# Chunked linear attention and a max-out feed-forward: the feed-forward of chunks 4 to 11 over two chunks at a time

## The chip, the cores and the metric

One NeuronCore of a Trainium2 chip runs the whole program in one launch. The engines are TensorE (PE, matmuls, with its weight loads shown apart as PEld), VectorE (DVE), ScalarE (ACT), GpSimd (POOL) and SyncE (SP), which here only issues transfers. The metric is the device time of one execution in microseconds, taken over several executions; lower is better.

## The reference, cut to what matters

```python
# r, k, v: (4, 8, 768, 48); w, u: (8, 48)
for t in range(768):
    cur = einsum('bhd,bhe->bhde', u * k[t], v[t])
    y[t] = einsum('bhd,bhde->bhe', r[t], state + cur)
    state = w[:, :, None] * state + einsum('bhd,bhe->bhde', k[t], v[t])
x = y as (4 * 768 tokens, 384)
h = maximum(maximum(x @ w1, x @ w2), x @ w3)      # 384 -> 768
out = h @ w_out                                   # 768 -> 384
```

The weights of the feed-forward come as float64 and everything else as float32.

## The kernel before, in words

The 768 steps are cut into 12 chunks of 64. A chunk holds 64 steps of 4 batches, 256 tokens (TOK), and is worked on in two halves q, each of four heads. Within a chunk the recurrence is written as matmuls: scores of k and r (`scores`), masked to earlier steps (`mask`); values (`values`), which add scores times v and r times the incoming state; keys (`keys`), which with `into_state` make the state of the next chunk. These operands are split into a high and a low float16 part, each product of two operands being three matmuls (`three`, L410, PSUM pool psa, 64 or 48 columns). The stationary operands are block-diagonal tiles (`Block`: kb, ktb, vb, sb) that a transfer from one SBUF tile to another spreads out (`spread`, L320 and L321). So each half chunk has loads (feat, tok), scaling on POOL or DVE (L367, L386, L406), splitting on ACT and DVE (L333, L338, L340), spreads, matmuls, and at the end x of the chunk: `x_high` (ACT, L466) and `x_low` (DVE, L471), two tiles xh and xl of 128 x 3 x 256 in the float32r form.

The feed-forward of a chunk (`ffn`) takes x = xh + xl and weights split likewise. For each of six slices f of the hidden columns and each of the three matrices i, `up` makes nine matmuls (three parts of the inner dimension times three products) into a PSUM tile of the pool psm (4 buffers): 18 groups of nine. `first` (ACT, L499) copies the group i = 0 to a tile m, `least` (DVE, L503) takes the maximum with groups 1 and 2, `h_high` (ACT, L506) and `h_low` (POOL or DVE, L512) split the result into hh and hl. `down` then makes 3 x 18 matmuls, `leaving` (ACT, L535) copies each of the three output tiles to a tile io, and ACT issues its store (L874). All feed-forward matmuls have line L488; a chunk has 162 + 54 = 216 of them with 256 columns.

At the start 16 half blocks of weight words (float64, 576 KB each, tiles raw64, 4 buffers) are loaded and converted by ACT and DVE to a high and a low part that stay in SBUF. Near the end the same words are loaded a second time (`again`, L698) and vetted: `vet_words` (DVE, L264) and `vet_sum` (ACT, L268) check that each lies in the range in which the fast conversion holds; `check`, `count` and `verdict` join all such checks, and a slow general path (`general`) would run after the fast one if any failed.

The order of the work on every engine is written out ahead by a planner, `Plan`. Each step is announced with `do`: an engine, a modelled cost, what it reads, writes and takes from a pool, and a due time in chunks. `order` then goes through a model of the five engines: the step that can start earliest goes first, and among those that can start at about the same time the one with the lower due time. The due times are moved by SHIFT, by kind of step ("act m": ACT steps that make m), with two values, for dues up to 1.6 and later. Attention of chunk c + 1 is due at c and the feed-forward of chunk c also at c. On the chip each engine keeps the order so found and waits where an operand isn't there. SP issues all loads and spreads, in order.

```python
plan = Plan(dict(feat=2, tok=3, raw64=4, psa=4, psm=4, ..., xh=2, xl=2, m=3, io=3, hh=1, hl=1))
...
order = plan.order(dict(pe=0.5, dve=5.2, act=3.0, pool=13.0, sp=1.6))
for p in order:
    p["fn"]()
```

Of the kernel before, what the change touches and what calls it, by code (L numbers as in the profile page):

```python
# [18 lines left out]
P = 128  # L19
B, H, S, D = 4, 8, 768, 48  # L20
C = 64
# [16 lines left out]
class Plan:  # L38
# [6 lines left out]
    OPENING = 1.6  # L45
    SHIFT = {
        "act ah": (-5.31, -0.9), "act am": (2.08, 0), "act hh": (1.37, 0.4), "act his": (-0.69, 0), "act io": (-5.36, -2.55),
        "act kb": (-1.33, 0), "act kdh": (-2.9, 1.2), "act ktb": (1.56, 0), "act ktdh": (2.65, 0.45), "act m": (0.81, -0.9),
        "act odd": (0, 0.6), "act rh": (1.04, -0.85), "act sdh": (-5.26, 2.75), "act sq": (-6.83, 0.2), "act state": (-3.36, 0),
        "act tkt": (-0.31, 0), "act vb": (-2.77, 0), "act vdh": (-3.65, 2.05), "act xh": (1.12, -1.45), "act ztop": (-4.35, 0),  # L50
        "dve a": (4.95, 2.4), "dve al": (5.58, 0.7), "dve am": (-3.84, 0.85), "dve ends": (0, 0.45), "dve flag": (0, -2),
        "dve good": (0, -3), "dve hl": (2.63, -2.25), "dve kT": (6.29, 0), "dve kdec": (8.61, 0), "dve kdl": (-1.52, -0.15),
        "dve ktdl": (-3.55, 1.1), "dve lo": (-4.52, 0), "dve m": (-2.24, 0.3), "dve rT": (9.32, 0), "dve rl": (-2.27, 0.75),
        "dve sdl": (3.31, -0.15), "dve state": (-2.75, 1.5), "dve vdl": (4.98, 0.55), "dve vet": (0, -0.15), "dve word": (-1.81, 0),
# [10 lines left out]
    def do(self, due, eng, cost, fn, reads=(), writes=(), takes=(), size=0, near=0):  # L65
# [6 lines left out]
        late = due > self.OPENING  # L72
        due += self.SHIFT.get(kind, (0, 0))[late]
# [8 lines left out]
        self.todo.append(dict(n=n, due=due, eng=eng, cost=cost, fn=fn, need=need, takes=takes, size=size, near=near, kind=kind, late=late, touch={*reads, *writes, *new}))  # L82
# [68 lines left out]
def kernel(ctx, tc, feat, tok, wu, ut, ws, wo, cst, out):  # L151
# [9 lines left out]
    wld = ctx.enter_context(tc.tile_pool(name="wld", bufs=4))  # L161
# [57 lines left out]

    def load_weight(n, h, shift=0):  # L220

        raw = wld.tile([P, 4 * HN + 4], I16, name="raw64")
        src = (ws[n] if n < NF else wo[n - NF]).bitcast(I16)
        nc.sync.dma_start(out=raw[:, shift:shift + 4 * HN], in_=src[:, h * 4 * HN:(h + 1) * 4 * HN])
        return raw

# [44 lines left out]
    pw = wld.tile([P, NP, C + 1], F32, name="raw64")  # L271
# [261 lines left out]
    def leaving(ps, n):  # L533
        o = tmp.tile([P, n], F32, name="io", bufs=3)
        nc.scalar.copy(out=o, in_=ps)  # L535
        return o

    def xtile(n):
        return [xp.tile([P, NJ, n], F32R, name=f"x{s}") for s in "hl"]
# [36 lines left out]
    def general():  # L576
# [60 lines left out]
        with tc.For_i(0, NCH // 2, 1) as i:  # L637
            for b in range(B):
                xt = wld.tile([P, NJ, P], F32, name="raw64")
# [13 lines left out]
                x = xtile(P)  # L653
# [15 lines left out]
    plan = Plan(dict(feat=2, tok=3, raw64=4, psa=4, psm=4, rh=2, rl=2, am=2, a=2, ah=1, al=1, xh=2, xl=2, m=3, io=3, hh=1, hl=1))  # L669
# [7 lines left out]
    def helping(c, columns):  # L677
        return ("pool", 0.05 + 2.5e-3 * columns) if c > 2 else ("dve", dve(columns))

    def dve(columns):  # L680
        return 0.07 + 1.05e-3 * columns
# [4 lines left out]
    def weight(n, h, due):  # L686
# [5 lines left out]
        dma(due, fetch, 8 * P * HN, takes=[("raw64", w)])  # L692
# [5 lines left out]
    def again(n, h, due):  # L698
        w = ("vet", n, h)

        def fetch():
            T[w] = load_weight(n, h)

        dma(due, fetch, 8 * P * HN, reads=[("begun", int(due))], takes=[("raw64", w)])
# [99 lines left out]
    def leave_x(c, q, due):  # L804
        def x_hi():
            if q == 0:
                T["x", c] = [xp.tile([P, NJ, TOK], F32R, name="xh"), None]
            x_high(c, q, T["x", c][0])

        def x_lo():  # L810
            if q == 0:
                T["x", c][1] = xp.tile([P, NJ, TOK], F32R, name="xl")
            x_low(c, q, *T["x", c])

        hi, lo = ("xh", c), ("xl", c)
        do(due + 0.03, "act", 0.6 if q == 0 else 1.55, x_hi, reads=[("va", c, q)], **(dict(takes=[("xh", hi)]) if q == 0 else dict(writes=[hi])))
        do(due + 0.04, "dve", 0.62 if q == 0 else 1.7, x_lo, reads=[("va", c, q), hi], **(dict(takes=[("xl", lo)]) if q == 0 else dict(writes=[lo])))
# [18 lines left out]
    def ffn(c):  # L836
        x = [("xh", c), ("xl", c)]
        for f in range(NF):
            due = c + 0.11 * f
            for i in range(3):  # L840
                def mul(f=f, i=i):
                    T["up", c, f, i] = up(T["x", c], f, i, TOK)
# [133 lines left out]
```

## Time and profile before

| what | value |
|---|---|
| time, median of 3 runs | 414.87 us (414.4 to 414.98) |
| profiled execution: span | 413.4 us; no other time is given for it |
| PE busy | 393.2 us, 95% |
| DVE, ACT, POOL busy | 283.6 (69%), 256.1 (62%), 183.2 us (44%) |
| moved by the DMA engines | 90.08 MB, 218 GB/s on average |
| granted TensorE clock, mean | 0.998 |

The span goes from the first to the last instruction of the program. PE's busy time is that of matmuls that overlap in the engine's pipeline, so the spacing of matmuls is read from the chain and from the timeline, in which equal neighbours are merged: "160.53 11.75 PE psm L488 x99" is a stretch that begins at 160.53 us, lasts 11.75 us and holds 99 matmuls. A row of a group gives the busy time, the mean duration in ns, then the engine's idle time ahead of it with what ended it. A row of waits gives the sum, how often, and the longest.

### The profile page before, as it was taken

Reading aid. Unit: us, or ns where it says so; the run is one execution under the profiler, and the core shown is the slowest. Engines: PE = TensorE matmul, PEld = TensorE weight load, DVE = VectorE, ACT = ScalarE, POOL = GpSimd, SP = SyncE. Lnnn points to the kernel's source line nnn. Section 1 sums busy time; section 2 is a strip of 40 time slices with the busy share of each in tenths; the row PEclk is TensorE's granted clock in tenths of the full one; section 3 lists DMA queues with packets and bytes.
Section 4 is the critical chain, followed back from the end, with each engine's and each line's share of the span. In section 5 each row is a group of like instructions: output and inputs, shape, how many; then the busy total and the mean of one; then the engine's idle time right before and its main releaser. Section 6 shows DMA issues by size and latency. Waiting matters only on the chain.

```text
span 413.4 us, 11975 instructions
## 1 busy us (share of the span) xinstructions
PE 393.2 (95%) x4758; PEld 388.5 (94%) x4758; DVE 283.6 (69%) x550; ACT 256.1 (62%) x674; POOL 183.2 (44%) x180
## 2 busy tenths in 40 slices
PE   2869999999999999999999999999999999999996
PEld 2759999999999999999999999999999999999995
DVE  6888999988688766767667666567676596354240
ACT  5999987885766556456456456466456477265231
POOL 9000000298668754674664654754574551020120
PEclk9999999999999999999999999999999999999999
DMA  7899998889799997786785786785885996886101
GB/s 286 320 314 212 255 307 285 223 224 293 207 276 239 248 226 186 224 225 158 226 223 139 247 214 162 233 222 148 239 222 142 310 301 148 243 304 203 38 2 41
DMA packets 30954, 90.08 MB, mean 218 GB/s; under 512 B 4784, under 2 KB 9648, under 8 KB 30896
## 3 DMA queue, kind: packets, MB, share of 16 engines
q1 hardware_dynamic: 25568, 84.47, 72.1%
q10 hardware_dynamic: 5328, 4.82, 3.7%
q8 instruction: 38, 0.62, 0.7%
q14 instruction: 20, 0.16, 0.2%
HBM read 45.85 MB, written 4.72 MB: 122 GB/s over the span
## 4 chain that ended last, share of the span: by engine, by line
PE 65%; DVE 3%; ACT 3%; DMA 2%; issue 1%; POOL 1%; ACTq 0%; SPq 0%; DVEq 0%
PE psm L488 55%; PE psa L410 10%; DMA sb<-sd 2%; ACT junk L350 1%; DVE kd L338 1%; DVE state L446 0%; ACTq L874 0%; DVE m L503 0%; ACT io L535 0%; ACT xh L466 0%; DVE am L420 0%; POOL feat L367 0%; DVE hl L512 0%; ACT kd L333 0%; DVE sd L340 0%
## 5 line engine op out<-in xcount | busy, mean ns | idle before, releaser
L488 PE MATMUL psm<-xh,wh 128*128 128x256 f32 x648 | 166.6, 287 | 4.9 <-ACT xh L466 2.9
L488 PE MATMUL psm<-xl,wh 128*128 128x256 f32 x648 | 163.6, 282 | 1.1 <-DVE xl L471 1.1
L488 PEld LDWEIGHTS psm<-xh,wh 128*128 128x128 f32 x648 | 123.4, 190 | 5.7 <-ACT xh L466 3.1
L488 PEld LDWEIGHTS psm<-xl,wh 128*128 128x128 f32 x648 | 123.0, 190 | 1.4 <-DVE xl L471 1.4
L488 PE MATMUL psm<-xh,wl 128*128 128x256 f32 x648 | 112.9, 284 | 0.0
L503 DVE TENSOR_TENSOR m<-psm,m 128x256 f32<-128x256 f32 x144 | 60.4, 420 | 63.2 <-PE psm L488 54.5
L488 PEld LDWEIGHTS psm<-xh,wl 128*128 128x128 f32 x648 | 93.1, 190 | 0.0
L367 POOL TENSOR_TENSOR feat<-feat,wrt 128x512 f32<-128x512 f32 x36 | 47.1, 1319 | 74.7 <-DVE sd L340 68.9
L512 POOL TENSOR_TENSOR hl<-m,hh 128x256 fp32r<-128x256 f32 x55 | 46.5, 847 | 73.8 <-ACT hh L506 73.7
L506 ACT CAST hh<-m 128x256 fp32r<-128x256 f32 x72 | 28.8, 404 | 57.0 <-DVE m L503 56.7
L488 PE MATMUL psm<-hh,woh 128*128 128x256 f32 x216 | 54.3, 284 | 0.0
L488 PE MATMUL psm<-hh,wl 128*128 128x256 f32 x216 | 53.4, 279 | 0.0
L386 POOL TENSOR_TENSOR am<-tok,u_sb 128x384 f32<-128x384 f32 x18 | 21.0, 1165 | 58.0 <-DVE al L430 58.0
L350 ACT ACTIVATE junk<-tok 128x384 bf16<-128x384 f32 x72 | 37.5, 520 | 14.6 <-DMA tok<-in_tok_dram 12.0
L488 PEld LDWEIGHTS psm<-hh,woh 128*128 128x128 f32 x216 | 40.6, 188 | 0.0
L488 PEld LDWEIGHTS psm<-hh,wl 128*128 128x128 f32 x216 | 40.6, 188 | 0.0
L471 DVE SCALAR_TENSOR_TENSOR xl<-psa,xh 32x256 fp32r<-32x256 f32 (+2 forms) x60 | 28.3, 471 | 14.5 <-ACT xh L466 13.6
L466 ACT ACTIVATE xh<-psa 32x256 fp32r<-32x256 f32 (+2 forms) x60 | 25.0, 417 | 16.4 <-PE psa L410 15.4
L488 PE MATMUL psm<-hl,woh 128*128 128x256 f32 x216 | 35.1, 280 | 0.0
L338 DVE TENSOR_TENSOR kd<-feat,kd 128x512 f16<-128x512 f32 x22 | 20.5, 933 | 19.6 <-ACT kd L333 19.6
L410 PE MATMUL psa<-ah,vb 128*128 128x64 f16 x352 | 32.9, 194 | 0.0
L410 PE MATMUL psa<-rh,sb 128*128 128x64 f16 x352 | 32.5, 193 | 0.0
(98 smaller groups left out, 742.0 us busy)
## 6 DMA issues: line engine op xcount, KB each, us to landing
tok<-in_tok_dram SPq DMA_DIRECT2D x24, 576.0 KB, 6.8
raw<-in_ws_dram SPq DMA_DIRECT2D x24, 576.0 KB, 7.4
feat<-in_feat_dram SPq DMA_DIRECT2D x24, 512.0 KB, 5.4
kb<-kd SPq DMA_DIRECT2D x22, 256.0 KB, 5.9
kb<-kd SPq DMA_DIRECT2D x22, 248.0 KB, 6.1
ktb<-ktd SPq DMA_DIRECT2D x20, 256.0 KB, 3.4
ktb<-ktd SPq DMA_DIRECT2D x20, 248.0 KB, 4.5
raw<-in_wo_dram SPq DMA_DIRECT2D x8, 576.0 KB, 5.5
```

The lines of the kernel that those rows point to most:

```text
L338: nc.vector.tensor_tensor(out=dense.dense[:, 1, :, 0:w], in0=src, in1=dense.dense[:, 0, :, 0:w], op=ALU.subtract)
L350: nc.scalar.activation(out=junk, in_=src, func=AF.Square, scale=scale, accum_out=stat[:, kind, 2 * c + q:2 * c + q + 1])
L367: helper(c).tensor_tensor(out=t[n], in0=t[n], in1=tb, op=ALU.mult)
L386: helper(c).tensor_tensor(out=w.rearrange("p (g b) d -> p g b d", g=2), in0=t["r"], in1=by_token(u_sb, q), op=ALU.mult)
L410: nc.tensor.matmul(out=ps, lhsT=l[i], rhs=rr[j], start=first and n == 0, stop=last and n == 2)
L466: nc.scalar.mul(out=hi, in_=src, mul=SC_X)
L471: nc.vector.scalar_tensor_tensor(out=lo, in0=src, scalar=SC_X, in1=hi.bitcast(F32), op0=ALU.mult, op1=ALU.subtract)
L488: nc.tensor.matmul(out=ps, lhsT=a, rhs=b, start=first and n == 0, stop=last and n == len(prods) - 1)
L503: nc.vector.tensor_tensor(out=to, in0=ps, in1=m, op=ALU.max)
L506: nc.scalar.copy(out=h[0][:, f, :], in_=m)
L512: lows_by(c, f).tensor_tensor(out=h[1][:, f, :], in0=m, in1=h[0][:, f, :].bitcast(F32), op=ALU.subtract)
```

## The change

Chunks 0 to 3 keep a feed-forward each. Chunks 4 and 5, 6 and 7, 8 and 9, 10 and 11 are joined to pairs (GROUPS): their feed-forward is done once over 512 columns. So for the pairs

- `up` and `down` make one matmul of 512 columns where there were two of 256; a PSUM tile of psm is then 2 KB wide;
- m, hh, hl and io have 512 columns, and `first`, `least`, `h_high`, `h_low`, `leaving` and the stores run once per pair. m and io have 2 buffers, before 3;
- xh and xl of a pair are one tile each, in the pool "big", which is the former pool of weight words (raw64, 4 buffers). Attention of both chunks writes into its part of the tile, so the first `up` of a pair reads x of both;
- the words for the vetting go to buffers of "tok" (3), which hold the attention's loads, and not to those of the weight words; a vetting load is gated by the beginning of the feed-forward of the pair in whose time it is due.

The planner's SHIFT has three values per kind (dues up to 1.6, up to 4, later), all of them new, attention of chunk c is due at `AT[c]`, the planner's costs of the matmuls are 0.1185 us at 256 columns and 0.2165 us at 512, and the scratch space for software-made transfer descriptors is set to 1024 bytes.

```diff
-    OPENING = 1.6
+    STAGES = (1.6, 4)
+    AT = (-1, 0.95, 1, 2.7, 1.4, 1.85, 5.25, 6.3, 4.5, 7.05, 8.25, 8.6)
...
-        "act ah": (-5.31, -0.9), "act am": (2.08, 0), "act hh": (1.37, 0.4), "act his": (-0.69, 0), "act io": (-5.36, -2.55),
+        "act ah": (-3.45, 16.4, 13.05), "act am": (12, 22.55, -27.25), "act hh": (0.95, 25.75, -6.3),
...
-        late = due > self.OPENING
-        due += self.SHIFT.get(kind, (0, 0))[late]
+        if kind in self.SHIFT:
+            due += self.SHIFT[kind][sum(due > t for t in self.STAGES)]
...
-    wld = ctx.enter_context(tc.tile_pool(name="wld", bufs=4))
+    big = ctx.enter_context(tc.tile_pool(name="big", bufs=4))
...
+    def load_again(n, h):
+        t = raw.tile([P, 4 * HN], I16, name="tok")
+        nc.sync.dma_start(out=t, in_=words_of(n, h))
+        return t
...
-        m = tmp.tile([P, n], F32, name="m", bufs=3)
+        m = tmp.tile([P, n], F32, name="m", bufs=2)
...
-        o = tmp.tile([P, n], F32, name="io", bufs=3)
+        o = tmp.tile([P, n], F32, name="io", bufs=2)
...
+    def xtile(name, n):
+        if n > TOK:
+            return big.tile([P, NJ, n], F32R, name="big")
+        return xp.tile([P, NJ, n], F32R, name=name)
...
+    GROUPS = ((0,), (1,), (2,), (3,), (4, 5), (6, 7), (8, 9), (10, 11))
+    group_of = {c: g for g in GROUPS for c in g}
+    plan = Plan(dict(feat=2, tok=3, big=4, psa=4, psm=4, rh=2, rl=2, am=2, a=2, ah=1, al=1, xh=2, xl=2, m=2, io=2, hh=1, hl=1))
...
-        dma(due, fetch, 8 * P * HN, reads=[("begun", int(due))], takes=[("raw64", w)])
+        dma(due, fetch, 8 * P * HN, reads=[("begun", group_of[int(due)][0])], takes=[("tok", w)])
...
     def leave_x(c, q, due):
+        g = group_of[c]
+        new = c == g[0] and q == 0
+        mine = slice((c - g[0]) * TOK, (c - g[0] + 1) * TOK)
...
-    def ffn(c):
-        x = [("xh", c), ("xl", c)]
+    def ffn(g):
+        c, n = g[0], len(g) * TOK
+        x = [("xh", g), ("xl", g)] + [(a, b, q) for a in ("xh", "xl") for b in g for q in range(2)]
+        rate = 0.1185 if len(g) == 1 else 0.2165
+
+        def at(part):
+            return c + len(g) * part
...
-    for c in range(NCH):
-        if c + 1 < NCH:
-            for q in range(2):
-                fetched(c + 1, q, c - 0.6 + 0.5 * q, ["kb", "ktb"] if c == 1 else [])
-            attend(c + 1, c)
-        ffn(c)
+    for c in range(1, NCH):
+        for q in range(2):
+            fetched(c, q, Plan.AT[c] - 0.6 + 0.5 * q, ["kb", "ktb"] if c == 2 else [])
+        attend(c, Plan.AT[c])
+    for g in GROUPS:
+        ffn(g)
...
-    nc = _bacc.Bacc("TRN2", target_bir_lowering=False, num_devices=1)
+    nc = _bacc.Bacc("TRN2", target_bir_lowering=False, num_devices=1, dynamic_dma_scratch_size=1024)
```

More of the change, by code (lines that the diff above doesn't have):

```diff
@@ L81, in do @@
         need.discard(n)
-        self.todo.append(dict(n=n, due=due, eng=eng, cost=cost, fn=fn, need=need, takes=takes, size=size, near=near, kind=kind, late=late, touch={*reads, *writes, *new}))
+        self.todo.append(dict(n=n, due=due, eng=eng, cost=cost, fn=fn, need=need, takes=takes, size=size, near=near, kind=kind, touch={*reads, *writes, *new}))
     def order(self, free):
@@ L652, in general @@
                     nc.tensor.transpose(out=ps[:, j], in_=xt[:, j], identity=ident)
-                x = xtile(P)
+                x = [xtile(n, P) for n in ("xh", "xl")]
                 nc.scalar.copy(out=x[0], in_=ps)
@@ L677, in helping, with pool @@
     def helping(c, columns):
-        return ("pool", 0.05 + 2.5e-3 * columns) if c > 2 else ("dve", dve(columns))
+        return ("pool", pool(columns)) if c > 2 else ("dve", dve(columns))
+    def pool(columns):
+        return 0.05 + 2.55e-3 * columns
     def dve(columns):
@@ L804, in leave_x, with part, place, held @@
     def leave_x(c, q, due):
+        g = group_of[c]
+        new = c == g[0] and q == 0
+        mine = slice((c - g[0]) * TOK, (c - g[0] + 1) * TOK)
+        def part(n):
+            return T[n, g][:, :, mine]
         def x_hi():
-            if q == 0:
-                T["x", c] = [xp.tile([P, NJ, TOK], F32R, name="xh"), None]
-            x_high(c, q, T["x", c][0])
+            if new:
+                T["xh", g] = xtile("xh", len(g) * TOK)
+            x_high(c, q, part("xh"))
         def x_lo():
[L811 to L817, printed above, removed]
+            if new:
+                T["xl", g] = xtile("xl", len(g) * TOK)
+            x_low(c, q, part("xh"), part("xl"))
+        def place(n):
+            return dict(takes=[(n if len(g) == 1 else "big", (n, g))]) if new else {}
+        def held(n):
+            return [] if new else [(n, g)]
+        do(due + 0.03, "act", 0.6 if q == 0 else 1.55, x_hi, reads=[("va", c, q), *held("xh")], writes=[("xh", c, q)], **place("xh"))
+        do(due + 0.04, "dve", 0.62 if q == 0 else 1.7, x_lo, reads=[("va", c, q), ("xh", c, q), *held("xl")], writes=[("xl", c, q)], **place("xl"))
     def attend(c, at):
@@ L870, in part @@
             bank = ("dn", c, m)
-            do(due, "pe", len(fs) * 0.358, lambda: down(T["h", c], m, fs, banks, TOK), reads=reads, **(dict(takes=[("psm", bank)]) if 0 in fs else dict(writes=[bank])))
+            do(due, "pe", len(fs) * 3 * rate, lambda: down(T["h", c], m, fs, banks, n), reads=reads, **(dict(takes=[("psm", bank)]) if 0 in fs else dict(writes=[bank])))
             if NF - 1 in fs:
-                do(due + 0.02, "act", act(TOK), lambda: do_tile(("io", c, m), leaving(banks[m], TOK)), reads=[bank], takes=[("io", ("io", c, m))])
-                dma(due + 0.03, lambda: nc.scalar.dma_start(out=out[m, :, c * TOK:(c + 1) * TOK], in_=T["io", c, m]), 131072, reads=[("io", c, m)], eng="act")
+                do(due + 0.02, "act", act(n), lambda: do_tile(("io", c, m), leaving(banks[m], n)), reads=[bank], takes=[("io", ("io", c, m))])
+                dma(due + 0.03, lambda: nc.scalar.dma_start(out=out[m, :, c * TOK:c * TOK + n], in_=T["io", c, m]), 512 * n, reads=[("io", c, m)], eng="act")
         most, rest = range(NF - 1), [NF - 1]
         for m, fs, due in ((0, most, 0.70), (1, most, 0.77), (0, rest, 0.83), (1, rest, 0.85), (2, range(NF), 0.87)):
-            part(m, fs, c + due)
+            part(m, fs, at(due))
     for q in range(2):
```

60 lines of the change are left out of this document (34 added, 26 removed), and 8 rows, old and new, of the table SHIFT.

## The prediction

> **What bounds the kernel now.** I read the page first: busy shares, the 40 slices, the chain that ended last.
>
> ```profile
> span 413.4 us, 11975 instructions
> ...
> PE   2869999999999999999999999999999999999996
> ...
> PE 65%; DVE 3%; ACT 3%; DMA 2%; issue 1%; POOL 1%; ACTq 0%; SPq 0%; DVEq 0%
> ```
>
> TensorE (PE) is full from the fourth slice on, and the chain is PE for 65% of the span. The chain in order of time then shows one chunk of the steady part: "psm" pieces are feed-forward matmuls, "psa" pieces are attention.
>
> ```profile
> 160.53 11.75 PE psm L488 x99
> 172.28 1.42 PE psa L410 x48
> 173.69 1.14 PE psm L488 x9
> 174.83 0.61 PE psa L410 x24
> 175.45 1.15 PE psm L488 x9
> 176.59 0.72 PE psa L410 x24
> 177.31 11.75 PE psm L488 x99
> 189.06 2.72 PE psa L410 x96
> 191.77 11.73 PE psm L488 x99
> ...
> 409.40 0.37 ACT io L535
> ```
>
> From 160.53 to 191.77 a chunk takes 31.24 us. Of it 1.42 + 0.61 + 0.72 + 2.72 = 5.47 us are attention, the other 25.8 us are 216 feed-forward matmuls; inside the long pieces one costs 11.75/99 = 118.6 ns for its 256 columns. After the last matmul only the copy, one store and 4 us remain. So from here on the time falls only if PE's own stream gets shorter, and rises if PE is made to wait.
>
> The other engines are not full, by the windows view (columns: stretch and length, busy us of PE, its weight loads, DVE, ACT, POOL, granted clock, share of the DMA engines, GB/s).
>
> ```profile
> 80.00:120.00 40.00, 37.86 (x540) 37.04 (x537) 32.37 (x53) 28.58 (x82) 30.34 (x26) 1.00 0.91 255
> 120.00:160.00 40.00, 39.84 (x545) 39.46 (x545) 27.07 (x50) 24.25 (x69) 28.95 (x27) 1.00 0.90 233
> 160.00:200.00 40.00, 40.00 (x498) 39.83 (x494) 29.28 (x59) 23.85 (x65) 23.02 (x21) 1.00 0.78 207
> 200.00:240.00 40.00, 40.00 (x555) 39.70 (x554) 26.62 (x48) 22.03 (x63) 22.64 (x22) 1.00 0.70 197
> ```
>
> Between 160 and 240 us DVE is 70% busy, ACT and POOL 57%, the DMA engines 74%. Before 160 us the DMA engines are at 0.90: the opening has little room.
>
> **The matmuls of the pairs.** For chunks 4 to 11 two matmuls of 256 columns become one of 512: 8 x 216 = 1728 become 864. No row has a 512-column matmul, so its price is bounded. If the time went by columns it would be 2 x 118.6 = 237.2 ns and nothing is saved. What speaks against that is the stretch in which PE ran slowly, just after its start (timeline of PE; the windows row has 1.00 as granted clock there, so that column does not show this slowness).
>
> ```profile
> 36.00:39.70 3.70, 3.70 (x19) 3.70 (x19) 0.00 (x0) 0.00 (x0) 1.00 0.86 194
> ...
> 37.75 0.41 PE L488 MATMUL psm<-xh,wh 128*128 128x256 f32 x1
> ...
> 39.03 0.84 PE L488 MATMUL psm<-xh,wl 128*128 128x256 f32 x3
> 39.67 0.40 PE L488 MATMUL psm<-xh,wh 128*128 128x256 f32 x1
> ```
>
> Nine matmuls from 37.75 to 39.67 are 213.3 ns each, 0.833 ns per column. If the fast rate were exactly twice that, 256 columns would take 106.7 ns, and 118.6 has 12 ns besides. These 12 ns are not added in the slow stretch (256 columns would have taken 225 there if it were the pure rate plus 12), so they look like something beside the columns that ends later than a short matmul and is covered by a long one. The weight load is such a thing, by the first matmuls of the timeline:
>
> ```profile
> 8.39 3.64 PE L483 MATMUL psa<-feat,kb 128*128 128x64 f32 x16 [2.08 <-DVE am L387]
> 12.95 2.79 PE L483 MATMUL psa<-am,vb 128*96 128x64 f32 x16 [0.91 <-DVE am L420]
> ```
>
> Both move 64 columns; the one with 128 weight columns takes 3.64, the one with 96 takes 2.79, a ratio of 1.30 against 1.33 for the weights. There the load sets the pace and the columns hide behind it. A 512-column matmul covers any such load that fits in 118.6 ns. Its own time is then 512 x 0.4167 = 213.3 ns, plus what the 64-column attention matmuls show over their columns (1.42 us/48 = 29.6 ns against 26.7): 2.9. I take 216 ns. Bounds: 213.3 and 237.2, with 225 (12 ns added whatever the length) between. Saved: 864 x (237.2 - 216) = **18.3 us**.
>
> The Trainium skill ("TensorE: Matmul & The Clock Gate", section "Back-to-back issue gap") gives a lone stream N/2.4 + 2.5 ns, which is 109.2 at 256 columns and 215.8 at 512: by it alone a pair would save only 2.5 ns, 2.2 us in all, which speaks against the change. The same section says that in a stream with weight loads both set the spacing. The trace has 118.6 at 256 and so disagrees with the lone-stream figure there; no run here yet shows 512.
>
> **What the pair must wait for.** Feed-forward of chunks 4 and 5 now starts when x of *both* is there. Before, it started on chunk 4 alone:
>
> ```profile
> 166.22 0.75 PE L488 MATMUL psm<-hl,woh 128*128 128x256 f32 x5
> 166.81 0.28 PE L488 MATMUL psm<-xh,wh 128*128 128x256 f32 x1
> ```
>
> At 166.81 chunk 3 ends and chunk 4 begins. Call S the start of the first pair. PE has nothing else by then but chunk 5's attention, of which the first scores are already done (a piece of 96 is 48 value, 24 key and 24 score products, the last ones of the next chunk; 0.7 us): 5.47 - 0.7 = 4.8 us. So PE alone allows S = 171.6. When is x of chunk 5 ready? The rows are the key products (once per half chunk) and the last part of x:
>
> ```profile
> 106.69 0.37 PE L410 MATMUL psa<-vd,ktb 128*128 128x48 f16 x8
> ...
> 128.19 0.39 PE L410 MATMUL psa<-vd,ktb 128*128 128x48 f16 x9
> ...
> 159.07 0.41 PE L410 MATMUL psa<-vd,ktb 128*128 128x48 f16 x10
> ...
> 161.83 1.74 DVE L471 SCALAR_TENSOR_TENSOR xl<-psa,xh 96x256 fp32r<-96x256 f32 x4
> ...
> 192.44 1.74 DVE L471 SCALAR_TENSOR_TENSOR xl<-psa,xh 96x256 fp32r<-96x256 f32 x4
> ```
>
> These are the second halves of chunks 2, 3, 4; x follows its key product by 161.83 + 1.74 - 159.07 = 4.5 us. From chunk 2 to 3 attention took 21.5 us, from 3 to 4 30.9, the rhythm of PE. So 21.5 is a pace that it can do. The transfers agree:
>
> ```profile
> q1 hardware_dynamic: 25568, 84.47, 72.1%
> ```
>
> 84.47 MB in 72.1% of 413.4 us is 283 GB/s while busy; a chunk moves 31.24 us x 202 GB/s (mean of 160 to 240) = 6.3 MB, which is 22.3 us at that rate. With 21.5 us from 128.19 on, chunk 5's keys come at 171.2 and its x at 175.7. I take **S = 176**. Bounds: 171.6, and 194.2 if attention keeps its old time. PE then waits 4.4 us; a wait of some us could bring the slow rate back: the stretch above, 3.7 us at half pace, cost 1.9. Against it stand chunk 6's first scores (0.72), done in the wait. I set both against each other: 0, bounds -0.7 and +1.9. The longest waits of PE in the whole run are these, both before 29 us:
>
> ```profile
> PE psa L296 <- DVE stat L346: 5.2, 1, 5.2
> PE psm L488 <- ACT xh L466: 2.9, 1, 2.9
> ```
>
> The Trainium skill (same page, "Part 1: The HAM clock gate") puts the return to half rate at an idle window of about 3.4 us; the trace, with half pace some us after waits of 5.2 and 2.9 us, does not contradict it.
>
> **The rest of the path.** From 166.81 to the end there were 246.6 us. Now from S: 246.6 - 18.3 (matmuls) - 4.8 (chunk 5's attention lies ahead of S) + 1.2 for the tail = 224.7. The tail: the copy of 0.37 (409.40 above) becomes some 0.55, +0.2; the last store has 128 KB more, at 283 GB/s 0.46; and the third copy now waits for the first store.
>
> ```profile
> out_dram<-io ACTq DMA_DIRECT2D x36, 128.0 KB, 3.9
> ```
>
> That store is issued about 1 us after its bank is full and lands 3.9 + 0.46 later, 5.4 in all; the third bank is full after 3 x 0.216 (second bank) + 18 x 0.216 = 4.5 us. 0.9 late at most, I take 0.5.
>
> **What costs nothing, and its cover.** Evacuation of PSUM gets fewer, wider instructions:
>
> ```profile
> L503 DVE TENSOR_TENSOR m<-psm,m 128x256 f32<-128x256 f32 x144 | 60.4, 420 | 63.2 <-PE psm L488 54.5
> L367 POOL TENSOR_TENSOR feat<-feat,wrt 128x512 f32<-128x512 f32 x36 | 47.1, 1319 | 74.7 <-DVE sd L340 68.9
> L512 POOL TENSOR_TENSOR hl<-m,hh 128x256 fp32r<-128x256 f32 x55 | 46.5, 847 | 73.8 <-ACT hh L506 73.7
> L506 ACT CAST hh<-m 128x256 fp32r<-128x256 f32 x72 | 28.8, 404 | 57.0 <-DVE m L503 56.7
> ```
>
> At 512 columns: ACT at most 0.81 (twice L506), POOL 1.32 to 1.69 (L367, twice L512), DVE at most 0.84 (twice L503), against 9 x 0.216 = 1.94 us for the group that fills a bank. With four banks a bank may come back 5.8 us late before PE stops. The ring of m goes from three to two: m(f) lives two groups (3.9) + 0.84 + 0.81 + 1.69 = 7.2 us, and is wanted again after six (11.7), with the banks behind it. Without that cover, the low part on POOL waiting behind four or more attention steps of 1.3 us, PE would lose about 1 us each time; 20 such steps bound it at 20 us. I take 0: POOL is idle 43% of the time, and DVE and ACT are relieved. The ring of io, also two now, is met only at a group's end, where the tail term below has it.
>
> In the steady part a pair period is 2 x 31.24 - 18.3/4 = 57.9 us for two chunks of attention, 29 each: the DMA share rises from 0.74 to 0.80, DVE from 70% to at most 75%. That fits, and x of the next pair goes to two other slots.
>
> The 16 vetting loads now take the three "tok" slots, ahead of chunk 10's and 11's tokens: a load waiting for a slot holds SP's queue, and behind it stand the spreads of kb, ktb, vb, sb, on which PE's attention waits.
>
> ```profile
> raw<-in_ws_dram SPq DMA_DIRECT2D x24, 576.0 KB, 7.4
> ...
> L268 ACT ACTIVATE raw<-raw,beyond 128x576 f32<-128x576 int32 x16 | 13.3, 829 | 4.4 <-DVE raw L264 3.6 <-ACT raw L268 0.8
> ```
>
> A load and its two passes hold a slot some 9 us, so three slots pass one per 3 us. Five loads are gated by pair 8/9, eleven by the last pair: 33 us inside its 47. I take 0; were the five all in the way, 15 us less the 12 us or so per pair by which attention (45 at 22.3 each) is quicker than 57.9: 3 us. The smaller DMA scratch bears on no transfer of this program that the queue table shows.
>
> **Sum.** Span: 176 + 224.7 = 400.7. The page gives the profiled execution no time but its span of 413.4; the runs' median of 414.87 lies 1.5 above, so **402.2 us**.
>
> **The rivals.**
> - *Attention does not get ahead (slower).* Its place is the start of the first pair; with x of chunk 5 where it was (192.44 + 1.74 = 194.2), 194.2 + 224.7 + 1.5 = 420.4. It decides from S = 413.4 - 224.7 = 188.7 on, where gain and wait cancel. For: DMA at 0.90 and DVE at 81% before 120 us. Against: 21.5 us between two chunks. A partial form, S at 181 to 187, gives 407.2 to 413.2.
> - *The matmul costs its columns (the change does not do what it says).* 237.2 ns: 402.2 + 18.3 = 420.5. For: 118.6 is not the half of 213.3. Against: the slow stretch and the weight-bound rows.
> - *12 ns stay on each matmul.* 225 ns: 402.2 + 864 x 9 ns = 410.0.
> - *The new dues shorten the opening* so that even S = 171.6 is undercut: the two waits above are 8.1 us; half or more of them recovered, with S at its floor, gives 171.6 - 4 (to 8) + 224.7 + 1.5 = 390 to 394.
>
> **How the numbers follow.** My forecast (395 to 406): 0.56. Shorter opening: 0.10. 225 ns: 0.07. Late pair, still faster: 0.08. Attention not ahead: 0.08. Cost by columns: 0.08. Within 0.2%, about what a measurement of this kernel can tell from no change: 0.03. Faster is 0.56 + 0.10 + 0.07 + 0.08 = 0.81, same 0.03, slower 0.16. The range 391 to 415 leaves out the two slower cases and little else.
>
> **What would show it.** The page of the changed kernel should have 864 matmuls of 128x512 in pieces of 99 lasting 21.4 us. S is the first of them: near 176 if right, 171 to 172 if attention is no limit, over 188.7 if I am wrong on the sign. A wait of PE behind xh or xl should stand there and nowhere later; a PE wait on m, io or hl in the pairs would break the zero for the rings, one on sb or vb after 290 us the zero for the vetting.

## The result, and the profile after

The changed kernel takes 427.20 us (median of 4 executions, 423.85 to 428.45) against 414.93 us for the kernel before on the same chip (414.40 to 415.96). The ratio is 1.027, with a 95% interval of 1.022 to 1.032: slower, where 402.2 us and a range of 391 to 415 had been forecast. The profiled execution took 428.08 us with a span of 426.3 us, so 1.8 us lie around the span and the change in span, +12.9 us, is nearly the change in time. Of the runs below, singles and lightact each had one execution that stands apart (637.85 us at a mean granted clock of 0.58, and 429.29 us, which is the profiled one); their ratios and medians leave it out.

In the changed kernel the feed-forward matmuls have line L504 (before L488) and those of attention L426 (before L410). These are the lines of its page that answer to those shown of before.

```profile
span 426.3 us, 10086 instructions
...
PE   3859989999689897989999999999999999999994
...
PE 61%; DMA 14%; ACT 10%; DVE 9%; issue 3%; SPq 2%; POOL 0%; ACTq 0%; DVEq 0%
...
L504 PE MATMUL psm<-big,wh 128*128 128x512 f32 x432 | 113.9, 399 | 0.0
```

The wide matmuls are there. The slices of PE have holes (8, 6, 8, 8, 7, 8) up to slice 18, about 190 us, where the kernel before had nines from the fourth on, and the share of DMA in the chain went from 2% to 14%.

The first pair starts at the last row of this piece of PE's timeline.

```profile
181.31 0.75 PE L504 MATMUL psm<-hl,woh 128*128 128x256 f32 x5
181.91 0.77 PE L426 MATMUL psa<-vd,ktb 128*128 128x48 f16 x24
...
183.95 0.19 PE L426 MATMUL psa<-rh,kb 128*128 128x64 f16 x1 [1.28 <-DMA kb<-kd]
...
184.65 1.65 PE L504 MATMUL psm<-big,wh 128*128 128x512 f32 x6
```

S is 184.65 us, with 171.6 as PE's floor. Chunk 3's feed-forward ends at about 181.9; before it ended at 166.8. About 3.6 of these 15 us are no loss but attention that is done earlier (1008 of its 2160 matmuls begin before the end of chunk 3, 888 in the kernel before). The lost time does not stand in one wait in front of the pair. It has been collected on the way, and the waits of PE show where. First the kernel before, from 76 to 166.9 us (columns: us in total, times, the longest):

```profile
PE psm L488 <- ACT io L535: 0.9, 2, 0.7
PE psa L410 <- DVE rl L377: 0.8, 1, 0.8
PE psm L488 <- ACT m L499: 0.3, 1, 0.3
PE psa L410 <- DVE al L430: 0.3, 1, 0.3
```

The same view of the changed kernel, from 76 to 184.6 us:

```profile
PE psa L426 <- DMA ktb<-ktd: 4.1, 3, 2.1
PE psa L426 <- DMA kb<-kd: 2.5, 3, 1.3
PE psa L426 <- ACT ktd L349: 2.5, 1, 2.5
PE psa L426 <- DMA sb<-sd: 1.9, 1, 1.9
PE psa L426 <- DMA vb<-vd: 1.2, 1, 1.2
```

It was 2.3 us before and is 12.2 us now, 9.7 of them for a spread that has not landed (ktb, kb, sb, vb). All stand at attention products. These waits are 9.9 of the 13 us by which S misses its floor; 0.8 us more is that feed-forward is seven matmuls behind at 76 us, and most of the rest lies in feed-forward cut into more and shorter pieces (123.2 ns for each of its matmuls from 76 us to S, 120.5 before). The windows agree (columns as in the prediction):

```profile
80.00:120.00 40.00, 35.31 (x501) 34.37 (x497) 28.27 (x50) 27.11 (x81) 30.32 (x27) 1.00 0.88 237
120.00:160.00 40.00, 35.98 (x513) 34.99 (x513) 29.06 (x50) 22.94 (x62) 24.58 (x23) 1.00 0.93 230
160.00:200.00 40.00, 36.24 (x427) 32.79 (x427) 33.17 (x57) 24.72 (x64) 25.04 (x22) 1.00 0.87 227
200.00:240.00 40.00, 39.53 (x463) 32.62 (x462) 35.98 (x53) 27.68 (x68) 31.85 (x24) 1.00 1.00 270
```

Between 80 and 200 us PE is busy for 36 of 40 us while the DMA engines are at 0.87 to 0.93. In the chain in order of time, long transfers stand between the pieces of PE up to S, and from 323.62 us on it is one single piece:

```profile
88.07 8.72 DMA tok<-in_tok_dram
101.37 8.18 DMA ktb<-ktd
...
119.99 7.66 DMA sb<-sd
130.11 10.20 DMA sb<-sd
...
147.83 5.49 DMA ktb<-ktd
156.54 8.28 DMA tok<-in_tok_dram
...
323.62 96.28 PE psm L504 x414
...
419.93 0.59 ACT io L551
```

That last piece prices the wide matmul inside the kernel: 96.28 us / 414 = **232.6 ns**, not 216. And it ends at 419.90, 6.4 us ahead of the end of the span; before, the copy began at 409.40, 4.0 us ahead of it.

The account of the span, before to after, +12.9 us:

| step | us |
|---|---|
| start of the first pair, 184.65 instead of the floor of 171.6 | +13.05 |
| matmuls of the pairs, 203.56 us in the trace instead of 206.24 | -2.7 |
| from the last matmul of the feed-forward to the end, 6.4 instead of 4.0 us | +2.4 |

The three make 12.75; what is left is rounding and where the last matmul is taken to end. The 203.56 us are 864 matmuls with all boundaries between pieces (235.6 ns each); the 206.24 are 1728 of the kernel before (119.35 each). From S to the end PE waits 0.4 us in all.

### The profile page after: what moved, and what is told of

It is laid out like the page before. It is cut to its first block, busy times and chain, and to the rows that moved or that the text cites. A ratio compares the mean times of both kernels' runs of the same rounds, so it can differ in the third digit from the quotient of the medians.

```text
span 426.3 us, 10086 instructions
## 1 busy us (share of the span) xinstructions
PE 391.4 (92%) x3894; PEld 343.6 (81%) x3894; DVE 288.8 (68%) x498; ACT 250.5 (59%) x614; POOL 186.1 (44%) x160
## 2 busy tenths in 40 slices
DMA packets 29219, 89.97 MB, mean 211 GB/s; under 512 B 4592, under 2 KB 6384, under 8 KB 29168
## 4 chain that ended last, share of the span: by engine, by line
PE 61%; DMA 14%; ACT 10%; DVE 9%; issue 3%; SPq 2%; POOL 0%; ACTq 0%; DVEq 0%
PE psm L504 51%; PE psa L426 9%; DMA tok<-in_tok_dram 6%; DMA sb<-sd 4%; DMA ktb<-ktd 3%; ACT junk L366 3%; DVE big L261 1%; DVE wl L268 1%; ACT ztop L257 1%; DVE m L519 1%; SPq L336 1%; ACT am L414 1%; PE psa L499 1%; SPq L337 1%; ACT kd L349 1%
## 5 line engine op out<-in xcount | busy, mean ns | idle before, releaser
L504 PE MATMUL psm<-big,wh 128*128 128x512 f32 x432 | 113.9, 399 | 0.0
L519 DVE TENSOR_TENSOR m<-psm,m 128x256 f32<-128x256 f32 (+1 forms) x96 | 53.1, 553 | 64.5 <-PE psm L504 59.7
L504 PEld LDWEIGHTS psm<-big,wh 128*128 128x128 f32 x432 | 79.7, 188 | 17.9
L504 PE MATMUL psm<-big,wl 128*128 128x512 f32 x216 | 61.5, 393 | 0.0
L504 PE MATMUL psm<-xh,wh 128*128 128x256 f32 x216 | 57.1, 293 | 0.0
L504 PE MATMUL psm<-xl,wh 128*128 128x256 f32 x216 | 55.7, 287 | 1.2 <-DVE xl L487 1.2
L504 PEld LDWEIGHTS psm<-big,wl 128*128 128x128 f32 x216 | 40.5, 188 | 9.6
L504 PE MATMUL psm<-hh,woh 128*128 128x256 f32 (+1 forms) x144 | 47.0, 343 | 0.0
L504 PE MATMUL psm<-hh,wl 128*128 128x256 f32 (+1 forms) x144 | 46.1, 336 | 0.0
L504 PEld LDWEIGHTS psm<-xl,wh 128*128 128x128 f32 x216 | 41.8, 193 | 1.7 <-DVE xl L487 1.7
L504 PEld LDWEIGHTS psm<-xh,wh 128*128 128x128 f32 x216 | 42.0, 194 | 0.0
L504 PE MATMUL psm<-xh,wl 128*128 128x256 f32 x216 | 38.0, 285 | 0.0
L426 PE MATMUL psa<-ah,vb 128*128 128x64 f16 x352 | 33.5, 193 | 1.2 <-DMA vb<-vd 1.2
L426 PE MATMUL psa<-rh,sb 128*128 128x64 f16 x352 | 32.5, 193 | 1.9 <-DMA sb<-sd 1.9
L426 PEld LDWEIGHTS <-vb 128*128 128x128 f16 x528 | 27.5, 98 | 6.3 <-issue 4.0
L426 PE MATMUL psa<-al,vb 128*128 128x64 f16 x176 | 31.3, 193 | 1.3 <-DVE al L446 1.1
```

The costliest lines, as they stand in the source:

```text
L426: nc.tensor.matmul(out=ps, lhsT=l[i], rhs=rr[j], start=first and n == 0, stop=last and n == 2)
L504: nc.tensor.matmul(out=ps, lhsT=a, rhs=b, start=first and n == 0, stop=last and n == len(prods) - 1)
L519: nc.vector.tensor_tensor(out=to, in0=ps, in1=m, op=ALU.max)
```

## The experiments

Two questions had to be told apart: what a 512-column matmul costs and why, and what holds the start of the first pair. In the table, "chunk 3" is the end of its feed-forward and S the start of the first pair in the profiled execution, in us; the ratio is to the kernel before on the same chip.

| run | median, us | ratio (95%) | chunk 3 | S | span |
|---|---|---|---|---|---|
| changed kernel | 427.20 | 1.027 (1.022 to 1.032) | 181.9 | 184.65 | 426.3 |
| split | 431.56 | 1.038 (1.035 to 1.041) | 181.5 | 183.95 | 428.1 |
| singles | 438.42 | 1.050 (1.045 to 1.056) | 180.9 | | 438.0 |
| olddues | 476.37 | 1.144 (1.140 to 1.149) | 176.0 | 188.86 | 475.0 |
| lightdma | 416.40 | 1.002 (0.999 to 1.004) | 171.2 | 172.48 | 413.2 |
| lightdve | 422.75 | 1.014 (1.008 to 1.019) | 178.0 | 180.08 | 420.8 |
| lightact | 424.05 | 1.017 (1.013 to 1.021) | 177.7 | 180.38 | 427.4 |
| recost | 443.71 | 1.066 (1.062 to 1.069) | 184.4 | 184.39 | 441.6 |
| earlycount | 424.12 | 1.021 (1.015 to 1.027) | 178.7 | 181.79 | 421.5 |
| oldlight | 415.75 | 1.000 (0.998 to 1.002) | 168.6 | | 415.1 |

S itself moves between executions: earlycount has the changed kernel's order on every engine up to 407 us, and its S is 2.9 us earlier (181.79). A single S is good to some 3 us, and a smaller difference says nothing.

### stream: the matmul alone

The fast path is replaced by bare series of matmuls on four PSUM buffers, with the operand's type and width as the only variables, each in groups of nine with nine weight tiles in turn.

```diff
+    runs = [("warm", "r", 256, 6), ("r256", "r", 256, 11), ("r512", "r", 512, 11), ("r384", "r", 384, 11), ("r128", "r", 128, 11), ("h64", "h", 64, 22), ("h128", "h", 128, 22), ("h256", "h", 256, 11), ("h512", "h", 512, 11), ("z256", "z", 256, 11), ("z512", "z", 512, 11), ("s256", "r", 256, 11), ("s512", "r", 512, 11)]
+    for name, kind, n, groups in runs:
+        for g in range(groups):
+            ps = psm.tile([P, n], F32, name="psm")
+            for k in range(9):
+                nc.tensor.matmul(out=ps, lhsT=weights[kind][:, k * P:(k + 1) * P], rhs=moving[name], start=k == 0, stop=k == 8)
```

> Leaves out the whole computation: only streams of matmuls with 128x128 weights from random data, nothing else running, each stretch of one form (float32r with 128, 256, 384, 512 columns; float16 with 64, 128, 256, 512; float32r on zeros with 256 and 512; float32r 256 and 512 once more at the end). Theory 1, the columns cost some 0.445 ns each at full speed whatever the type: float32r 512 at 230 to 235 ns, 384 at 175, 256 at 118; float16 512 at 228 to 232; zeros the same. Theory 2, only the float32r stream is slow: float16 512 at 214 to 217, float32r 512 at 232. Theory 3, the data slow it (power): zeros at 512 at 214 to 217. Theory 4, something else in the kernel (transfers, other engines) slows it: float32r 512 at 216 here.

PE's timeline merges neighbours with the same weights' tile, so a row holds several widths under the shape of its first:

```profile
8.18 8.67 PE L73 MATMUL psm<-warm,wr 128*128 128x256 f32 x54 [8.18 <-ACT warm L64]
16.69 62.70 PE L73 MATMUL psm<-r,wr 128*128 128x256 f32 x396
79.23 49.18 PE L73 MATMUL psm<-h,wh 128*128 128x64 f16 x594
128.05 35.11 PE L73 MATMUL psm<-z,wz 128*128 128x256 f32 x198
163.00 35.06 PE L73 MATMUL psm<-s,wr 128*128 128x256 f32 x198
```

From start to start of the single matmuls inside these rows, in ns, with what is left after the columns at 0.4167 ns each:

| type | 64 | 128 | 256 | 384 | 512 columns |
|---|---|---|---|---|---|
| float16 | 29.2 | 55.8 | 109.2 | | 215.8 |
| float16, beyond the columns | 2.5 | 2.5 | 2.5 | | 2.5 |
| float32r | | 111.7 | 120.0 | 173.6 | 226.8, later 232.4 |
| float32r, beyond the columns | | 58.4 | 13.3 | 13.6 | 13.5, later 19.1 |

Zeros (row z) and data (row s) take the same: 99 matmuls of 256 and 99 of 512 columns in 35.1 us each. So a float32r matmul has a fixed part of some 12 to 14 ns at 256, 384 and 512 columns alike (zeros at 256 columns take 118.7); at 512 columns a second rhythm has 19. A longer matmul does not cover it, the data do not cause it, and nothing else of the kernel does: from 16 us on the other engines are idle here, and the share of the DMA engines is at most 0.01. 128 columns stand apart. The weight load may set their pace, for which the section on the prediction has a row; no run varied it at that width. The 216 ns hold for float16 only. The Trainium skill's N/2.4 + 2.5 ns ("TensorE: Matmul & The Clock Gate", section "Back-to-back issue gap") agrees with the float16 row to 0.1 ns and is 11 ns or more too low for float32r on data.

In the first row PE is still slow; its single spacings are 213 to 214 ns, as in the kernel before: at half pace the 13 ns are not there at 256 columns, the only width that ran so. The prediction had read this absence as cover.

### stream2: is it the weight load?

The same series with fewer weight columns, since the prediction had named the weight load as what lies behind the 12 ns.

```diff
-                nc.tensor.matmul(out=ps, lhsT=weights[kind][:, k * P:(k + 1) * P], rhs=moving[name], start=k == 0, stop=k == 8)
+                nc.tensor.matmul(out=ps, lhsT=weights[kind][:, k * P:k * P + w], rhs=moving[name], start=k == 0, stop=k == 8)
```

> Leaves out the whole computation: bare matmul streams again, float32r on random data with 128, 64 or 32 weight columns (512 moving: 128, 64, 32; 384: 64; 256: 128, 64, 32; 448: 128; 512 with 128 three times in all) and float16 512 with 32. If what a float32r matmul takes beyond its columns is its weight load, it shrinks with the weight columns: 512 at 227 to 232 with 128, about 220 with 64, 216 to 218 with 32; 256 at 120, 113, 110. If it is a fixed cost of each float32r matmul, the spacing stays at 227 to 232 and 120 whatever the weights.

PE's timeline; "128*64" is a weight tile of 64 columns:

```profile
17.34 18.55 PE L73 MATMUL psm<-a,wr 128*128 128x512 f32 x81
35.72 18.79 PE L73 MATMUL psm<-b,wr 128*64 128x512 f32 x81
54.35 18.92 PE L73 MATMUL psm<-c,wr 128*32 128x512 f32 x81
73.11 14.20 PE L73 MATMUL psm<-d,wr 128*64 128x384 f32 x81
87.15 9.88 PE L73 MATMUL psm<-e,wr 128*128 128x256 f32 x81
96.87 9.35 PE L73 MATMUL psm<-f,wr 128*64 128x256 f32 x81
106.06 9.34 PE L73 MATMUL psm<-g,wr 128*32 128x256 f32 x81
115.33 17.66 PE L73 MATMUL psm<-i,wh 128*32 128x512 f16 x81
...
151.45 16.57 PE L73 MATMUL psm<-k,wr 128*128 128x448 f32 x81
167.86 18.54 PE L73 MATMUL psm<-l,wr 128*128 128x512 f32 x81
```

From the start of one row to the next over 81, with 64 or 32 instead of 128 weight columns a wide matmul is not cheaper (a 226.9, b 230.0, c 231.6 ns). Only at 256 columns does a narrower load take something off (e 120.0, f 113.5). 448 columns cost 202.6 ns (k), 16 beyond the columns. The weight load isn't the cause of the fixed part at 512; at 256 it is about half of it. Why 512 columns take 226.8 ns in some series and 230.0 to 232.4 in others stays open.

### split: the width alone

The order, the buffers and the evacuation of the changed kernel, with each wide matmul as two of 256 columns.

```diff
-        for n, (a, b) in enumerate(prods):
-            nc.tensor.matmul(out=ps, lhsT=a, rhs=b, start=first and n == 0, stop=last and n == len(prods) - 1)
+        for k in range(0, ps.shape[1], TOK):
+            w = min(TOK, ps.shape[1] - k)
+            for n, (a, b) in enumerate(prods):
+                nc.tensor.matmul(out=ps[:, k:k + w], lhsT=a, rhs=b[:, k:k + w], start=first and n == 0 and k == 0, stop=last and n == len(prods) - 1 and k + w == ps.shape[1])
```

> The changed kernel with each matmul of 512 columns made as two of 256 into the halves of the same bank, same order of steps. If a matmul costs its columns, the pairs get 2 to 4 us slower in all and the time is 429 to 431 us. If 512 columns are slowed by something of their own (a full bank, the wide tile), two halves at 118.6 ns are no slower: 424 to 427 us. By my prediction's price for 512 columns (216 ns) it would have been 18 us slower: 445.

431.56 us (430.03 to 432.7), by the first of the three readings. The pairs' matmuls take 207.43 us, 120.0 ns each, against 203.56 us in the changed kernel. The width is worth **3.9 us** here and not 18.3.

### singles: the new order without pairs

```diff
-    GROUPS = ((0,), (1,), (2,), (3,), (4, 5), (6, 7), (8, 9), (10, 11))
+    GROUPS = tuple((c,) for c in range(NCH))
```

> The changed kernel with every chunk a group of its own: new due times, two buffers for m and io, vetting in the tok slots, but no pair. If the opening was lost to the new order of the work, feed-forward of chunk 3 still ends near 180 us and the time is 424 to 430 us. If it was lost to the pair's need of chunk 5's x ahead of time, it ends near 167 to 172 and the time is 414 to 419 us.

435.66 to 439.76 us. Chunk 3 ends at 180.9 us, a microsecond from the changed kernel's 181.9 and 14 later than before, with the same 1008 attention matmuls ahead of it: the order with the new dues costs the opening its time whether or not there are pairs. Two buffers for m and io and the vetting in the slots of tok stay in this run, but PE's waits up to there are again on spreads (9.0 of 9.7 us), not on these. Its later part is slower too, so this run prices only the opening.

### olddues: pairs in the order before

The old dues, attention of chunk c due at c - 1, and one rule that keeps two pairs from opening at a time.

```diff
-    STAGES = (1.6, 4)
-    AT = (-1, 0.95, 1, 2.7, 1.4, 1.85, 5.25, 6.3, 4.5, 7.05, 8.25, 8.6)
+    STAGES = (1.6,)
+    AT = tuple(range(-1, 11))
...
-                do(due + 0.035 * i, "pe", 9 * rate, mul, reads=[*x, ...
+                do(due + 0.035 * i, "pe", 9 * rate, mul, reads=[*x, *([("done", b)] if f and b is not None else []), ...
```

> The changed kernel with the old due times (attention of chunk c due at c - 1, the two old values per kind), pairs kept; one more rule keeps the matmuls of a group's second slice behind the group before, so that the banks suffice. If the new due times cost the opening, the first pair starts before 180 us and the time is 415 to 422. If the pair's wait is the cost whatever the dues, the old dues, under which x of chunk 5 was ready at 194 us, start the pair at 190 to 200 us and the time is 430 to 440.

476.37 us, which neither reading had. Chunk 3 ends at 176.0 and the first pair starts at 188.86 us, 0.2 from where the prediction put the break-even, but then PE waits again at later pairs, from 190 us to the end:

```profile
PE psa L418 <- DMA vb<-vd: 11.5, 1, 11.5
PE psa L418 <- ACT ah L433: 9.5, 4, 3.2
PE psa L418 <- DMA kb<-kd: 4.8, 2, 3.7
PE psm L496 <- DVE big L479: 3.2, 3, 1.2
...
```

Each pair needs two new chunks of attention at once, and in the old order the second comes late at all three later pairs (PE is busy for 12.9 of 20 us from 240 us on, 8.9 of 15 from 320, 3.5 of 15 from 400); the mean granted clock falls to 0.93 with it. Of these two orders, the one that doesn't draw attention ahead is the slower, and the changed kernel pays for drawing it ahead in the opening.

### lightdma and oldlight: do transfers pace the opening?

Each `spread` makes two transfers. From a block's second use on, the second moves an eighth of its bytes; the number of transfers stays, and the rest of the block holds old values. 74.48 MB are moved instead of 89.97. In oldlight the same is done to the kernel before.

```diff
+    spreads = []
...
-        eng.dma_start(out=dst.flat[C:P, by:], in_=src.flat[C:P, 0:2 * U * src.w - by])
+        n = U * src.w // 4 if dst in spreads else 2 * U * src.w - by
+        spreads.append(dst)
+        eng.dma_start(out=dst.flat[C:P, by:by + n], in_=src.flat[C:P, 0:n])
```

> The changed kernel, same order and same number of transfers, but from the second use of each block on the second transfer of a spread moves only an eighth of its bytes (results differ). If the transfers pace the opening, feed-forward of chunk 3 ends, and the first pair starts, 8 to 12 us earlier (182 and 185 in the changed kernel become 172 to 176) and the time is 415 to 419. If the engines pace it, the start moves by less than 3 us and the time is 424 to 428.

> A control: the kernel before, with the second transfer of a spread at an eighth of its bytes from each block's second use on (results differ). If transfers pace only the new order of the opening, the kernel before, where PE is full, gains less than 2 us: 413 to 415. If transfers hold the old opening up as well, feed-forward of chunk 3 ends at 163 or earlier and the time is below 412.

lightdma's windows, then its timeline of PE at the first pair:

```profile
80.00:120.00 40.00, 38.32 (x532) 37.26 (x531) 29.27 (x55) 29.50 (x89) 32.25 (x27) 1.00 0.76 208
120.00:160.00 40.00, 40.00 (x593) 39.59 (x591) 33.13 (x60) 27.81 (x77) 30.90 (x27) 1.00 0.72 189
```

```profile
172.48 1.65 PE L508 MATMUL psm<-big,wh 128*128 128x512 f32 x6
```

With fewer bytes S falls from 184.65 to 172.48 us, 0.9 above PE's floor, and PE is full from 120 us on. The kernel before gains nothing from the same edit (ratio 1.000). So transfers pace the new opening and not the old one; whether it is the time of the single spread or the load on the DMA engines, this edit doesn't tell apart, as it cuts both. A third candidate is the order of SP's queue. In the changed kernel SP itself waits between 76 and 184 us, most of all with a load of feat (L185) for a buffer that DVE still reads, and the spreads behind it wait too:

```profile
SPq L185 <- DVE kd L354: 17.7, 3, 6.6
```

One of these waits lasts from 105.7 to 111.2 us. The DMA engines are nearly empty in it (shares of 0.09 and 0.04 in the two stretches of 2 us from 108 us on). Then 12 transfers are issued within 9 us, the share is 0.97 or more from 114 to 120 us, and PE waits 1.2 us for a spread of vb. So bytes over bandwidth is not the whole of it. In lightdma this wait is still 13.6 us, so it doesn't hold S up by itself; no run varied it alone.

The other reading is as plain: without the wait the changed kernel takes 416.40 us, ratio 1.002. The pairs then only draw level: 2.7 us won by the width, and 2.2 lost at the end (its last copy begins at 406.95 us, 6.2 ahead of the end, before 4.0).

### lightdve and lightact: do the engines pace it too?

DVE makes the low parts of k, v and the state for two of eight units; ACT reads two of eight units for the sums of squares.

```diff
-            nc.vector.tensor_tensor(out=dense.dense[:, 1, :, 0:w], in0=src, in1=dense.dense[:, 0, :, 0:w], op=ALU.subtract)
+            nc.vector.tensor_tensor(out=dense.dense[:, 1, 0:2, 0:w], in0=src[:, 0:2], in1=dense.dense[:, 0, 0:2, 0:w], op=ALU.subtract)
```

```diff
-        nc.scalar.activation(out=junk, in_=src, func=AF.Square, scale=scale, accum_out=stat[:, kind, 2 * c + q:2 * c + q + 1])
+        nc.scalar.activation(out=junk[:, 0:2], in_=src[:, 0:2], func=AF.Square, scale=2 * scale, accum_out=stat[:, kind, 2 * c + q:2 * c + q + 1])
```

> The changed kernel, same order, but DVE makes the low parts of k, v and the state for two of eight units only (results differ). If DVE's work in the order of the opening is what delays it, the first pair starts at 172 to 178 and the time is 414 to 421. If transfers or the order of the transfers are the cause, the start stays at 182 or later and the time at 424 or more.

> The changed kernel, same order, but ACT's sums of squares read two of eight units (the sums are scaled; the check of the ranges is weaker so). This takes 0.25 to 0.3 us off each of 94 instructions. If ACT paces the opening, the first pair starts 6 us or more earlier, time 417 to 421; if not, 183 to 185 and 425 to 428.

S comes to 180.08 and 180.38 us, 4.6 and 4.3 earlier, a third of what the lighter transfers give; but earlycount, whose opening is that of the changed kernel, is 2.9 earlier too, so most of this can be chance. The ratios are firmer: 1.014 (1.008 to 1.019) for DVE lies clear below the changed kernel's 1.022 to 1.032, that for ACT (1.013 to 1.021) just below it. So less work on DVE, and perhaps on ACT, helps, and neither brings S to its floor. That a spread that starts sooner lands sooner, in one chain (split on DVE or ACT, spread, product), would explain it; it is argued, not shown.

### recost: the plan with measured prices

The planner had 0.2165 us for a wide matmul. Here it has 0.235, 0.1195 for 256 columns, and higher ones for DVE and ACT, with the same dues.

```diff
-        return 0.07 + 1.05e-3 * columns
+        return 0.08 + 1.2e-3 * columns
...
-        return 0.11 + 0.83e-3 * columns
+        return 0.12 + 0.95e-3 * columns
...
-        rate = 0.1185 if len(g) == 1 else 0.2165
+        rate = 0.1195 if len(g) == 1 else 0.235
```

> The changed kernel with other prices in the planner: 0.235 us for a matmul of 512 columns, 0.1195 for 256, DVE 0.08 us + 1.2 ns a column (was 0.07 + 1.05), ACT 0.12 + 0.95 (was 0.11 + 0.83). Due times as they are. If the opening was lost because the order was made for faster engines, an order made for these prices starts the first pair at 176 to 182 and the time is 416 to 423. If the order matters little, 183 to 187 and 425 to 430.

443.71 us, so this was a miss. The first pair starts at 184.39, no sooner, and PE now waits in the later part as well (12 us after 190). These dues are worse with the true prices than with the ones they were made for; whether a plan with true prices and dues of its own would do better was not tried.

### earlycount: the end

The two matmuls that count the vetted words (on PE, "pe count") are due earlier.

```diff
-        ... "pe count": (52.5, -22.6, 11.95),
+        ... "pe count": (52.5, -22.6, -40),
```

> The changed kernel with the count of the checks ahead of the last output matmuls, not behind them; nothing else in the order changes. If the late verdict is what lengthens the tail (6.5 us from the last matmul to the end, 4.0 before), the tail becomes 4.0 to 4.8 and the time 425 to 426. If the wider store and copy make the tail, it stays at 6 or more and so does the time, 427.

In the changed kernel the count stands behind the last matmul, and the copy, the flag on DVE and the last store follow together (timeline):

```profile
419.82 0.19 PE L585 MATMUL psa<-good,ones 128*1 128x1 f32 x2
419.93 0.59 ACT L551 COPY io<-psm 128x512 f32<-128x512 f32 x1 [3.28 <-PE psm L504]
420.05 0.14 DVE L589 TENSOR_SCALAR flag<-psa 1x1 int32<-1x1 f32 x1 [10.56 <-PE psa L585]
420.78 0.34 ACTq L915 DMA_DIRECT2D out_dram<-io  x1
```

In earlycount:

```profile
417.44 0.59 ACT L551 COPY io<-psm 128x512 f32<-128x512 f32 x1 [3.56 <-SPq L955]
418.06 0.34 ACTq L915 DMA_DIRECT2D out_dram<-io  x1
```

From the copy to the end of the span it is 421.5 - 417.44 = 4.1 us instead of 426.3 - 419.93 = 6.4; from the last matmul of the feed-forward it is 4.4 instead of 6.4. So 2.0 to 2.3 us of the end were the place of the count, which the change's dues had moved. The last store shows where: it lands 2.02 us after its issue here and 4.06 in the changed kernel. The 3 us of the medians, 424.12 against 427.20, are from two chips with overlapping intervals, and S differs by as much between the two profiles, so they prove less than the row.

## Why the prediction was wrong, step by step

**The matmuls of the pairs: wrong, and this cost the sign.** The step read 118.6 ns as 106.7 plus 12 that a longer matmul would cover, on the ground that the slow stretch did not have the 12. stream shows 12 to 19 ns at every width from 256 up at full pace, and none at half pace, where only 256 columns ran, so absence at half pace says nothing on cover. Of the 16.6 ns between 216 and the 232.6 of the kernel, 10.8 are this part that stays (226.8 in the first series); the other 5.8 are the second rhythm, whose cause is open. The Trainium skill ("TensorE: Matmul & The Clock Gate", section "Wait — 56ns, not 53.3ns?") says of its 2.5 ns that they show only at the full array clock; the runs here show the same of the larger part of float32r, and that was the third reading, which the prediction lacked. The term was 18.3 us; it measured 2.7, or 3.9 with the order held fixed. The second leg was the two L483 rows that made the weight load the thing to cover. The rows were read rightly, and a third form of that line in the kernel before agrees:

```profile
20.32 3.19 PE L483 MATMUL psa<-tok,ktb 128*112 128x48 f32 x16 [0.70 <-issue]
```

From start to start these matmuls take 213, 187 and 160 ns with 128, 112 and 96 weight columns, 1.67 ns for each weight column, whether 64 or 48 columns move. But they are float32 at half pace (one load of 128 weight columns has a duration of 333 ns there, as in the slow row of stream, and some 190 at full pace). By that figure a load of 128 weight columns takes 213 ns at half pace, exactly as long as 256 columns, so the slow stretch could not tell load from columns; at twice the pace it would be some 107 ns (an estimate from these rows), near the 111.7 ns of 128 columns of float32r in stream. What fell with stream2 is the step from there to 512 columns: the load is hidden behind them, and the fixed part is there all the same.

**The rivals on this price.** "12 ns stay" had the mechanism: 225 ns against 226.8 in the first series, but 232.6 in the kernel. "It costs its columns" had the better number for the kernel (237.2) for a reason that is wrong: 384 columns would take 178 by it and took 173.6. Together they had 0.15.

**The start of the first pair: inside its bounds, but mis-sized.** 176 was taken, 184.65 measured, in 171.6 to 194.2: the wait was 13 us instead of 4.4. The step took the 21.5 us between two key products as a pace that attention can keep, and supported it with 6.3 MB per chunk at 283 GB/s, the rate of busy DMA engines. The prediction's own windows from 80 to 160 us have 255 and 233 GB/s, and those of the changed kernel 237 and 230, at which 6.3 MB take 27 us. lightdma shows that the transfers were the limit, though not whether by this rate, by the time of a single spread or by the order in SP's queue. The rival with attention not ahead decided from 188.7 on, and S stayed under it: by the prediction's own path the time would have been 184.65 + 224.7 + 1.5 = 410.9, still faster.

**The break-even itself.** From S to the end the changed kernel takes 426.3 - 184.65 = 241.65 us, not 224.7. To tie with 413.4, S would have to be 171.75, PE's floor. So with the true price an opening at PE's floor would only have drawn level, as lightdma does. To be faster, the change would also have needed an earlier floor (the prediction's rival of a shorter opening, 4 to 8 us) or a mended end (2 us).

**The tail: size off, cause wrong.** 1.2 us were forecast, 2.4 measured. The ring of io was not it; the count of the vetted words had come behind the last matmul, and earlycount gives back 2.0 to 2.3. That leaves 0.1 to 0.4 us for the wider copy and store, so the terms that the step did have were too large, and the one that mattered was missing.

**The zeros: right.** After S PE waits 0.4 us in all in the profiled execution, so neither the rings of m and io nor the vetting in the slots of tok nor the wider evacuation cost PE anything there. That the slow rate would not return fits too: the wide matmuls average 235.6 ns from S on, where 512 columns at the 0.833 ns of the slow stretch would be 427.

**The chances.** Of the 0.81 on faster, all but the 0.07 for 225 ns rested on one price that no row showed, argued from two indirect readings.

## What to carry to other kernels

A price that no row shows should be given its largest bound as a serious case, above all when the whole gain is that price: ask whether the sign survives it before adding up the rest. A cost that vanishes at half clock need not be one that a longer instruction covers. When work is drawn ahead into an opening, divide its bytes by the rate that the windows of that opening show, not by the rate of engines while busy, and look at what the queue that issues the transfers waits for. And where two executions of one order differ by 3 us at a mark, an experiment that moves the mark by 4 needs the times of many executions beside it.

## What was not expected of the hardware

- A float32r matmul with 128 weight columns costs 12 to 19 ns beyond its columns at full rate where float16 costs 2.5, at every width measured from 256 to 512 and whatever the data; at half rate none of it shows (213 to 214 ns at 256 columns). Two rhythms, 226.8 and 232.4 ns at 512 columns, each lasted through whole series; the cause is open.
- At half rate the spacing of the float32 matmuls of 48 and 64 columns goes with their weight columns, not with the columns that move: 213, 187 and 160 ns at 128, 112 and 96 weight columns.
- Two float32r matmuls of 256 columns and one of 512 differ by only 8 to 13 ns in bare series (240.0 against 226.8 to 232.4), and by 4.5 in the kernel (3.9 us over 864, by split).
- The last store landed 4.06 us after its issue in the changed kernel, while equal stores at 415.7 and 416.7 us took 2.0. Reading the flag is not what slows it: in earlycount the flag is read at 405.1 us, and the stores of 412.91 and 413.91 us take 4.45 and 4.08, just behind a branch in PE's queue at 412.81, while the last one takes 2.02. The changed kernel has this branch at 420.82 beside the store at 420.78, and the kernel before has it at 407.12 with stores of 3.67 and 3.15 us behind it and then one of 1.84. That the branch is the cause was not tested by itself.
